# x + alpha * fx: other piece sizes, fx ahead of x, other buffer homes, the first store issued earlier

## The chip, the core and the metric

The kernel runs on one core of a Trainium2 chip. The metric is the device time of one execution in microseconds; the kernel before has a median of 150.96 us in 3 runs (150.96 to 151.07).

## What is computed

```python
B, S, D = 512, 32, 640
x, fx : bfloat16 [512, 32, 640]      alpha : bfloat16 [1]

def reference(x, fx, alpha):
    return x + alpha * fx
```

Two inputs of 20.97 MB are read and one output of 20.97 MB is written. There is one multiplication and one addition for each element.

## The kernel before

Each of the three large arrays is seen as 128 rows of 160 KiB, one row for each partition of the on-chip memory (SBUF). All pieces are counted in units of 1 KiB of such a row (K = 512 bfloat16 elements), so a row has N = 160 units. A piece of *n* units is one DMA with 128 rows of *n* KiB. In the trace each row of a DMA is one packet on one of 16 DMA engines, so each engine moves 8 rows of each DMA.

The on-chip buffer `buf` (L72 before and after) has ALL = 207 units. Both inputs together have 320 units, so they don't fit at once and places are used again.

- `X` and `F` list the pieces of x and fx as (first unit, end). In the kernel before, piece i of x always lies in `buf` at its own units, and piece j of fx at `HOME[j]`. Later pieces overwrite places where a fx piece has been used up.
- `C` lists the compute steps. A step multiplies its part of fx by alpha in place (VectorE `tensor_scalar`, L99) and adds it to x in place (VectorE `tensor_tensor`, L107). `CUT` cuts the addition of step 5 into a first part of 1 unit and the rest.
- `S` lists the stores: 64, 64 and 32 units.
- `PLAN` is an order written out by hand, in which instructions are issued. Loads, alpha's load and stores are all issued by SyncE (SP) on one DMA queue, so that a load that must wait for VectorE holds up everything that SP issues behind it. VectorE carries out its own instructions in PLAN's order too.
- `LATE` adds one wait by hand: store 0 is not issued before the first part of compute step 5.
- alpha is loaded as one element (third DMA), spread to 128 partitions by one small matmul, and copied to `a_f` by VectorE, which the multiplications use.

Five large loads (8, 56, 64, 30 and 49 units) and alpha are issued without a wait. The four loads behind them wait until VectorE has used up what they overwrite.

Of the kernel before, what the change touches and what calls it, by code (L numbers as in the profile page):

```python
# [1 line left out]

# [4 lines left out]

ACT = mybir.ActivationFunctionType
ALU = mybir.AluOpType
F32 = mybir.dt.float32  # L10
BF16 = mybir.dt.bfloat16

K = 512
P = 128

X = [(0, 8), (8, 64), (64, 94), (94, 126), (126, 160)]  # L20
F = [(0, 64), (64, 113), (113, 140), (140, 160)]
HOME = [94, 158, 160, 187]
C = [(0, 32), (32, 64), (64, 66), (66, 93), (93, 113), (113, 140), (140, 160)]
CUT = {5: 114}
S = [(0, 64), (64, 128), (128, 160)]
N = 160
ALL = 207

PLAN = """
x 0  # L30
x 1
a
f 0
x 2
f 1
c 0
x 3
c 1
c 2
x 4  # L40
c 3
f 2
c 4
f 3
c 5
c 6
s 0
s 1
s 2
"""  # L50
LATE = {("s", 0): ("c", 5)}


@with_exitstack
def kernel(
    ctx: ExitStack,
    tc: tile.TileContext,
    x: bass.AP,
    fx: bass.AP,
    alpha: bass.AP,  # L60
    out: bass.AP,
):
    nc = tc.nc
    xv = x.flatten_outer_dims().rearrange("(p n) d -> p (n d)", p=P)
    fxv = fx.flatten_outer_dims().rearrange("(p n) d -> p (n d)", p=P)
    ov = out.flatten_outer_dims().rearrange("(p n) d -> p (n d)", p=P)
    assert xv.shape[1] == N * K

    consts = ctx.enter_context(tc.tile_pool(name="consts", bufs=1))
    psum = ctx.enter_context(tc.tile_pool(name="psum", bufs=1, space=bass.MemoryType.PSUM))  # L70
    whole = ctx.enter_context(tc.tile_pool(name="whole", bufs=1))
    ctx.enter_context(tc.manual_schedule())  # L72

    sync = mybir.DependencyInfo(mybir.DependencyClass.Sync, mybir.DependencyReason.DATA)
    buf = whole.tile([P, ALL * K], x.dtype, name="buf")
    moved = {}
    done = []

    def transfer(what, out, in_):
        r = nc.sync.dma_start(out=out, in_=in_)  # L80
        if what in LATE:
            tc.add_manual_dep(r.ins, moved[LATE[what]].ins.name, sync, reason="issue late")
        moved[what] = r
        done.append(r)

    def load_x(i):
        a, b = X[i]
        transfer(("x", i), buf[:, a * K : b * K], xv[:, a * K : b * K])

    def load_f(j):  # L90
        (a, b), h = F[j], HOME[j]
        transfer(("f", j), buf[:, h * K : (h + b - a) * K], fxv[:, a * K : b * K])

    def compute(i):
        a, b = C[i]
        j = next(j for j, (s, e) in enumerate(F) if s <= a and b <= e)
        h = HOME[j] + a - F[j][0]
        term = buf[:, h * K : (h + b - a) * K]
        nc.vector.tensor_scalar(  # L99
            out=term, in0=term, scalar1=lanes["a_f"][:], scalar2=None, op0=ALU.mult  # L100
        )
        ends = [a, CUT.get(i, b), b]
        for s, e in zip(ends, ends[1:]):
            if s < e:
                term = buf[:, (h + s - a) * K : (h + e - a) * K]
                total = buf[:, s * K : e * K]
                r = nc.vector.tensor_tensor(out=total, in0=total, in1=term, op=ALU.add)  # L107
                moved.setdefault(("c", i), r)
                done.append(r)

    def store(i):
        a, b = S[i]
        transfer(("s", i), ov[:, a * K : b * K], buf[:, a * K : b * K])

    lanes = {}

    def alpha_to_lanes():
        a_1 = consts.tile([1, 1], alpha.dtype, name="a_1")
        transfer("a", a_1[:], alpha[None, :])
        ones = consts.tile([1, P], alpha.dtype, name="ones")  # L120
        nc.vector.memset(ones[:], 1.0)  # L121
        a_ps = psum.tile([P, 1], F32, name="a_ps")
        done.append(nc.tensor.matmul(a_ps[:], ones[:], a_1[:], start=True, stop=True))  # L123
        lanes["a_f"] = consts.tile([P, 1], F32, name="a_f")
        nc.vector.tensor_copy(out=lanes["a_f"][:], in_=a_ps[:])  # L125

    does = {"x": load_x, "f": load_f, "c": compute, "s": store, "a": alpha_to_lanes}
    for step in PLAN.split("\n"):
        if step:
            what, *of = step.split()  # L130
            does[what](*map(int, of))

    rest = nc.sync.nop(nofuse=True)
    for i in done[:-1]:
        tc.add_manual_dep(rest.ins, i.ins.name, sync, reason="all but the last store")


# [1 line left out]
_INS = ['x', 'fx', 'alpha']  # L139
_OUTS = [((512, 32, 640), 'bfloat16')]  # L140


# [23 lines left out]
```

## Time and profile before

| what | value |
|---|---|
| median of 3 runs | 150.96 us |
| span of the profiled execution | 149.4 us (149.42 in the trace) |
| outside the span (150.96 - 149.42) | 1.54 us |
| bytes moved | 62.92 MB, mean 421 GB/s over the span |
| time of packets on the 16 DMA engines | 97.9% of the span |
| VectorE busy | 66.6 us, 45% |

The trace has a record of every packet (start, duration, bytes). The table puts those of each DMA together, in the order of issue. "Floor" is the shortest duration of one row of that size in that DMA; "excess" is what all 128 rows took above the floor, divided by 16 engines; "longer" counts the rows that took over 20 ns more than the median of that DMA; "first" and "last" are when the first and the last of the 16 engines had finished its share, in us from the start of the span.

| DMA | KiB a row | floor, ns | excess, ns | longer | first engine done | last engine done |
|---|---|---|---|---|---|---|
| x 0 | 8 | 307 | 430 | 32 | 4.52 | 4.87 |
| x 1 | 56 | 2116 | 42 | 7 | 21.45 | 21.82 |
| fx 0 | 64 | 2418 | 13 | 1 | 40.80 | 41.20 |
| x 2 | 30 | 1138 | 42 | 11 | 49.88 | 50.51 |
| fx 1 | 49 | 1851 | 64 | 4 | 64.69 | 65.70 |
| x 3 | 32 | 1213 | 21 | 5 | 74.37 | 75.42 |
| x 4 | 34 | 1288 | 72 | 11 | 84.77 | 85.71 |
| fx 2 | 27 | 1022 | 62 | 7 | 92.95 | 93.88 |
| fx 3 | 20 | 761 | 30 | 5 | 99.16 | 99.95 |
| store 0 | 64 | 2418 | 98 | 23 | 118.87 | 119.27 |
| store 1 | 64 | 2418 | 41 | 0 | 138.23 | 138.59 |
| store 2 | 32 | 1213 | 24 | 0 | 147.94 | 148.27 |

How to read it: eight rows times the floor is the least time in which one engine can do its share of a DMA; the differences of the last column are the time that it took on whichever engine was last. The first row of the first DMA starts at 1.75 us, and the span ends 1.15 us after the last row.

### The profile page before, as it was taken

How to read it: one execution, taken by the hardware profiler on the slowest of the kernel's cores; microseconds unless marked ns; L12 is line 12 of the kernel's file. 1: busy time of each engine (PE TensorE's matmuls, PEld its weight loads, DVE VectorE, ACT ScalarE, POOL GpSimd, SP SyncE). 2: the span in 40 equal slices, each digit the busy share in tenths (PEclk: the TensorE clock that was granted, in tenths of full speed). 3: DMA queues.
4: the chain of work that ended last, by engine and by line, in shares of the span. 5: the costliest groups of instructions: out<-in, count | busy, mean ns of one | idle time of the engine just before them, and what ended most of it. 6: DMA issues, size and time to landing. Idle time of an engine off the chain costs nothing.

```text
span 149.4 us, 89 instructions
## 1 busy us (share of the span) xinstructions
PE 0.2 (0%) x1; PEld 0.1 (0%) x1; DVE 66.6 (45%) x17; POOL 0.2 (0%) x4
## 2 busy tenths in 40 slices
PE   0000000000000000000000000000000000000000
PEld 0000000000000000000000000000000000000000
DVE  0000000000089999999999970799994000000000
POOL 0000000000000000000000000000000000000000
DMA  5996996969899999979989999999696969696993
GB/s 184 588 445 292 491 526 281 561 298 544 379 428 395 548 430 443 416 312 447 470 382 419 431 451 417 433 495 544 298 561 281 561 281 561 281 561 281 509 465 149
DMA packets 1730, 62.92 MB, mean 421 GB/s; under 512 B 194, under 2 KB 194, under 8 KB 194
## 3 DMA queue, kind: packets, MB, share of 16 engines
q1 hardware_dynamic: 1730, 62.92, 97.9%
HBM read 41.94 MB, written 20.97 MB: 421 GB/s over the span
## 4 chain that ended last, share of the span: by engine, by line
DVE 38%; DMA 36%; issue 2%; SPq 1%; DVEq 0%
DMA buf<-in_fx_dram 36%; DVE buf L107 24%; DVE buf L99 13%; SPq L80 1%; DVEq L99 0%
## 5 line engine op out<-in xcount | busy, mean ns | idle before, releaser
L107 DVE TENSOR_TENSOR buf<-buf 128x16384 bf16<-128x16384 bf16 (+5 forms) x8 | 43.9, 5492 | 0.2
L99 DVE TENSOR_SCALAR buf<-buf,a_f 128x16384 bf16<-128x16384 bf16 (+3 forms) x7 | 22.8, 3264 | 24.9 <-DMA buf<-in_fx_dram 24.9
L125 DVE COPY a_f<-a_ps 128x1 f32<-128x1 f32 x1 | 0.2, 159 | 21.3 <-PE a_ps L123 21.3
L121 DVE MEMSET ones<- 1x128 bf16 x1 | 0.2, 165 | 0.8 <-PEq L150 0.8
L123 PE MATMUL a_ps<-a,ones 1*128 1x1 bf16 x1 | 0.2, 158 | 22.1 <-DMA a<-in_alpha_dram 22.1
L150 POOL MEMSET const-bfloat16-1.0<- 128x1 bf16 x1 | 0.1, 102 | 0.0
L150 POOL MEMSET const-uint8-127<- 128x1 uint8 x1 | 0.1, 102 | 0.0
L123 PEld LDWEIGHTS <-ones 1*128 1x128 bf16 x1 | 0.1, 100 | 1.0 <-DVE ones L121 1.0
L150 POOL MEMSET const-float32-0.0<- 128x1 f32 x1 | 0.1, 99 | 0.2 <-issue 0.2
L150 POOL MEMSET const-float32-1.0<- 128x1 f32 x1 | 0.1, 99 | 0.0
## 6 DMA issues: line engine op xcount, KB each, us to landing
buf<-in_x_dram SPq DMA_DIRECT2D x1, 7168.0 KB, 21.0
buf<-in_fx_dram SPq DMA_DIRECT2D x1, 6272.0 KB, 63.2
buf<-in_x_dram SPq DMA_DIRECT2D x1, 4352.0 KB, 16.9
buf<-in_x_dram SPq DMA_DIRECT2D x1, 4096.0 KB, 20.8
out_dram<-buf SPq DMA_DIRECT2D x1, 4096.0 KB, 34.8
buf<-in_x_dram SPq DMA_DIRECT2D x1, 3840.0 KB, 48.5
buf<-in_fx_dram SPq DMA_DIRECT2D x1, 3456.0 KB, 14.0
buf<-in_fx_dram SPq DMA_DIRECT2D x1, 2560.0 KB, 11.8
```

What stands on the lines that cost most here:

```text
L80: r = nc.sync.dma_start(out=out, in_=in_)
L99: nc.vector.tensor_scalar(out=term, in0=term, scalar1=lanes["a_f"][:], scalar2=None, op0=ALU.mult)
L107: r = nc.vector.tensor_tensor(out=total, in0=total, in1=term, op=ALU.add)
L121: nc.vector.memset(ones[:], 1.0)
L123: done.append(nc.tensor.matmul(a_ps[:], ones[:], a_1[:], start=True, stop=True))
L125: nc.vector.tensor_copy(out=lanes["a_f"][:], in_=a_ps[:])
L150: nc = _bacc.Bacc("TRN2", target_bir_lowering=False, num_devices=1)
```

## The change

The pieces, the order and the places in `buf` are new; the arithmetic, the number of DMAs (9 loads, alpha, 3 stores) and the stores' sizes stay.

- x is loaded in 64, 32, 32, 32 units, fx in 8, 56, 32, 32, 32. Each piece carries its own home as a third number, for x too.
- The first two DMAs load fx (8 and 56 units) in place of x; x's first 64 units come behind them.
- Six loads of 32 units follow in the order fx, x, fx, x, fx, x. The first two of them wait for nothing. The other four wait for an addition that uses up the place they overwrite: fx 3 for the total of 32 to 64, x 2 for 0 to 32, fx 4 for 79 to 96, x 3 for 111 to 128.
- VectorE multiplies 64, 32, 32 and 32 units and adds in 7 pieces (32, 32, 17, 15, 17, 15, 32 units).
- `LATE` is gone. Store 0 stands in SP's order behind x 3, and waits for nothing that SP has not waited for already.

```diff
-X = [(0, 8), (8, 64), (64, 94), (94, 126), (126, 160)]
-F = [(0, 64), (64, 113), (113, 140), (140, 160)]
-HOME = [94, 158, 160, 187]
-C = [(0, 32), (32, 64), (64, 66), (66, 93), (93, 113), (113, 140), (140, 160)]
-CUT = {5: 114}
+F = [(0, 8, 96), (8, 64, 104), (64, 96, 160), (96, 128, 128), (128, 160, 175)]
+X = [(0, 64, 0), (64, 96, 64), (96, 128, 96), (128, 160, 143)]
 S = [(0, 64), (64, 128), (128, 160)]
 N = 160
 ALL = 207
 
 PLAN = """
+f 0
+f 1
+a
 x 0
+f 2
 x 1
-a
-f 0
+m 0 64
+t 32 64
+t 0 32
+f 3
 x 2
-f 1
-c 0
+m 64 96
+t 79 96
+f 4
+t 64 79
+m 96 128
+t 111 128
 x 3
-c 1
-c 2
-x 4
-c 3
-f 2
-c 4
-f 3
-c 5
-c 6
+t 96 111
+m 128 160
+t 128 160
 s 0
 s 1
 s 2
 """
-LATE = {("s", 0): ("c", 5)}
...
+    def units(v, a, b):
+        return v[:, a * K : b * K]
+
+    def at(pieces, a, b):
+        s, _, h = next(p for p in pieces if p[0] <= a < p[1])
+        e, _, g = next(p for p in pieces if p[0] < b <= p[1])
+        assert h - s == g - e
+        return units(buf, a + h - s, b + h - s)
...
+    def multiply(a, b):
+        term = at(F, a, b)
+        done.append(
+            nc.vector.tensor_scalar(
+                out=term, in0=term, scalar1=lanes["a_f"][:], scalar2=None, op0=ALU.mult
+            )
+        )
...
+    def total(a, b):
+        s = at(X, a, b)
+        done.append(nc.vector.tensor_tensor(out=s, in0=s, in1=at(F, a, b), op=ALU.add))
...
+    def store(i):
+        a, b = S[i]
+        done.append(nc.sync.dma_start(out=units(ov, a, b), in_=at(X, a, b)))
```

(m a b is `multiply`, t a b is `total`; f, x, s and a are the loads, the stores and alpha as before.)

## The prediction

> **What bounds the kernel now.** I began with the page's head and its DMA rows.
>
> ```profile
> span 149.4 us, 89 instructions
> PE 0.2 (0%) x1; PEld 0.1 (0%) x1; DVE 66.6 (45%) x17; POOL 0.2 (0%) x4
> ...
> q1 hardware_dynamic: 1730, 62.92, 97.9%
> HBM read 41.94 MB, written 20.97 MB: 421 GB/s over the span
> ```
>
> VectorE (DVE) works less than half of the span; the one DMA queue is occupied for 97.9% of it. What is left to the queue is 2.1%, some 3.1 us. Stretches cut where DMAs end show where it is:
>
> ```profile
> 0.00:1.74 1.74, 0.00 (x0) 0.10 (x1) 0.17 (x1) 0.20 (x4) 1.00 0.00 0
> ...
> 148.28:149.40 1.12, 0.00 (x0) 0.00 (x0) 0.00 (x0) 0.00 (x0) 1.00 0.00 0
> ...
> 40.80:99.20 58.40, 0.00 (x0) 0.00 (x0) 51.62 (x13) 0.00 (x0) 1.00 1.00 431
> 99.45:147.90 48.45, 0.00 (x0) 0.00 (x0) 14.41 (x3) 0.00 (x0) 1.00 1.00 431
> ```
>
> The last two numbers are the DMA share and GB/s. Nothing moves for the first 1.74 us or the last 1.12; in between the engines are full, in the loads as in the stores. (Packets are counted whole where they start, so only long stretches can be compared.) Then the timeline, for whether the queue ever waits for its issuer:
>
> ```profile
> 54.89 14.58 SPq L80 DMA_DIRECT2D buf<-in_x_dram  x2
> ...
> 80.27 8.65 SPq L80 DMA_DIRECT2D buf<-in_fx_dram  x2
> ...
> 98.60 15.66 SPq L80 DMA_DIRECT2D out_dram<-buf  x3
> ```
>
> The second number spans from the first issue of the group to the end of its last. x 3 is issued at 54.89, before fx 1 ahead of it has finished (65.70 in the table by DMA); fx 2 at 80.27, x 4 ends at 85.71. Store 0 is issued at 98.60, when the first engine finishes its loads at 99.16, and its first rows start at 99.44: here alone some engines stand still. The chain of waits explains VectorE's order only; it ends at 113.9, 35 us before the span, with the additions:
>
> ```profile
> 105.57 2.81 DVE buf L99
> 108.38 0.02 issue
> 108.40 5.49 DVE buf L107
> ```
>
> So the end is set by the bytes: on each engine 96 rows, one behind the other. The floors in the table lie on one line: 64 and 32 KiB differ by 2418 - 1213 = 1205 ns, 37.66 ns per KiB, and 1213 - 32 x 37.66 = 8 ns go to each row; 20 KiB gives 761 by this line, as measured. An engine's whole floor is 480 KiB x 8 x 37.66 ns = 144.6 us plus 96 x 8 ns = 0.8, together 145.4; the first row starts at 1.75 and the span ends 1.15 after the last, together 148.3. The span of 149.42 has only 1.1 us above that, which bounds any gain.
>
> **Where this 1.1 us is.** About 0.66 us lies in the first DMA: 1.75 to 4.87 is 3.12 us, 8 rows of 307 are 2.46. From fx 0's end to the last store's, the last engine needs 148.27 - 41.20 = 107.07; eight times the floors of those nine DMAs (1138, 1851, 1213, 1288, 1022, 761, 2418, 2418, 1213) is 106.58. So 0.49 us are lost. By the column of the last engine, x 2 takes 9.31 against 9.10 and fx 1 15.19 against 14.81, together 0.59 above the floor; the rest are between 0.02 under and 0.02 over. The engines, 0.40 apart at 41.20, are 1.01 apart at 65.70: single rows take up to 276 ns longer, on some engine. This befalls the loads of 30, 49, 34, 27 and 20 KiB (excess 42, 64, 72, 62, 30 ns) more than those of 64 (13) and 32 KiB (21).
>
> **The change, part by part.**
>
> 1. *Startup.* The first two DMAs have 8 and 56 KiB rows as before, alpha is third, a 64 KiB load fourth. fx for x is the same shape: 0. All are issued before 3.4 us and the last engine is done with them at 41.20 again; bounds -0.1 to +0.1, from the spread of the three runs (0.11).
> 2. *Row sizes.* Behind that, before: 30+49+32+34+27+20 = 192 units in six loads; after: six of 32. Bytes, rows and DMAs are the same, so the floors are as well: 58.20 and 58.20. What can change is the loss. x 3, the one 32 KiB load of the trace, cost the last engine 75.42 - 65.70 = 9.72. Six such: 41.20 + 6 x 9.72 = 99.52 against 99.95: **-0.43 us**. Lower bound: no loss at all, 6 x 9.70, -0.55. Upper bound: every one loses as x 2 did (0.21), 6 x 9.91 = 59.46, end at 100.66, +0.71. I take x 3's own row, because it has the size.
> 3. *Store 0 without LATE.* It is issued behind x 3, far ahead of need (below). The gap goes away: engines done at 99.16 waited until 99.44. But the last engine, done at 99.95, went on at once, and it is the one that ends the kernel, so 0; bounds -0.12 (the idle time summed over 16 engines and divided by 16, if they shared their rate) and +0.05 (their wait also brought the engines closer together).
> 4. *New homes and waits.* They cost nothing while each load is issued before the one ahead has ended. VectorE by its rows: 16384 elements take 4.48 us in L99 and 8.69 in L107, 10240 take 2.88 and 5.49; by these lines a multiplication of 32768 takes 8.76, additions of 8704 and 7680 take 4.69 and 4.16 (estimates). A DMA's data were seen 0.45 us after its last row (41.20, L99 starts at 41.65).
>    - The multiplication of 0 to 64 waits for fx at 21.82 and for a_f at 22.5: done at 31.3, long before x 0 (41.20).
>    - Additions 32-64 and 0-32 end at 50.3 and 59.0. fx 3 is issued at 50.4 (x 1 ahead of it ends at 60.6), x 2 at 59.1 (fx 3: 70.4).
>    - Multiplication 64-96 to 63.5, addition 79-96 to 68.2: fx 4 is issued at 68.3 (x 2: 80.1). Addition 64-79 to 72.4, multiplication 96-128 to 76.9.
>    - Addition 111-128 waits for x 2 (80.1 + 0.45) and ends at 85.2; x 3 is issued then, its first row could start 1.0 later (at the start 0.73 to 1.75), and fx 4 ends at 89.8. This cover, 3.6 us, is the thinnest. Queued behind x 3 on SP are all three stores.
>    - Store 0 is issued at 85.7 (x 3: 99.5), store 1 after addition 96-111 at 89.4 (store 0 ends at 118.8), store 2 after the last addition, 100.0 + 8.7 = 108.7 (138.2).
> 5. *Fewer VectorE instructions*, 4 + 7 for 7 + 8: by the lines above 66.0 us for 66.6. Hidden: VectorE ends at 108.7, its last result is needed at 138.2. 0.
>
> Sum: the last row ends at 99.52 + 19.32 + 19.32 + 9.68 = 147.84 for 148.27, the span is 147.84 + 1.15 = 148.99, -0.43. With the 1.54 us that lie between span and median, **150.53 us**; its own range is 150.40 to 150.70.
>
> **Rivals.**
>
> *A: the stretched rows don't depend on the size (no change, 150.96).* They came with the first VectorE work at 41.65, and fx 0, x 1 and the stores, with few of them, lie mostly outside that work; then the same bytes of VectorE work stretch the new rows as well, 0.49 us again. Against it: between 88.56 and 94.29 VectorE was idle, and 3 of the 79 rows wholly in idle stretches behind 41 us were longer, by 291 ns together (3.7 ns for each of the 79); of 641 rows wholly beside its work 37, by 2932 (4.6 each). The two are close. The Trainium skill (SBUF — State Buffer, "SBUF: two separate sides") says that a DMA can't be slowed by a compute operation, as the two use separate ports; this trace agrees, by 3.7 against 4.6 ns, and by that rule A loses its VectorE half. What is left of A is chance: a few long rows that fall on any engine at any size.
>
> *B: aligned rows disturb each other (slower, 151.7).* All loads now start and end at multiples of 32 KiB of their rows but for the first cut; if engines in step then hit the same memory at once, each of the six loads loses what x 2 did, 0.21: the upper bound above, +0.71, 151.67. It turns to a loss once each load loses over (99.95 - 41.20 - 58.20) / 6 = 0.09. For it: the losses are already there and not understood. Against: fx 0 and store 1, at 0 and 64 KiB with the engines in step, have 1 and 0 longer rows. The Trainium skill (DMA: Bandwidth & Descriptors, "Latency and other measured facts") tells of copies that lose half of their rate where the rows lie a large power of two apart; here rows lie 160 KiB apart before and after, and no run here shows such a loss.
>
> *C: the queue runs dry before x 3 (slower, 151.6).* If addition 111-128 or what precedes it ends over 3.6 us later, all engines stand still for the rest; with that addition at twice its time (+4.7) 1.1 us, less the 0.43: 151.6. Against: all additions of the trace lie on one line, at 8.69 and 5.49.
>
> **How the numbers follow.** Forecast 0.55, A 0.25, B 0.12, C 0.08. A measurement of this kernel can tell 0.2%, 0.30 us, from no change: the borders are 150.66 and 151.26. The forecast stays under 150.66 in some nine of ten (0.50), else it counts as the same (0.05). A lies within in four of five (0.20), with 0.02 faster and 0.03 slower; B and C are slower (0.20). Together 0.52, 0.25 and 0.23. The range runs from 150.30, just under the lower bounds together (-0.55 and -0.12), to 151.30, which takes in A; outside are most of B and C and little at the lower end, under 0.2.
>
> **What would show it.** Right: last-engine ends near 99.5 for x 3 and 147.8 for store 2, the engines no more than 0.6 us apart at the end of each load, few rows over 20 ns longer, store 0's rows starting the moment x 3's end, x 3 issued near 85. Wrong: excess over 40 ns per 32 KiB load (A), over 0.09 us on the last engine in each (B), or an idle stretch of all engines about 90 us (C); also a startup that ends elsewhere than at 41.2.

## The result and the profile after

The changed kernel takes 151.67 us (median of 5 runs, 151.53 to 151.81), the kernel before 151.04 us beside it: a ratio of 1.0039, 95% interval 1.0027 to 1.0051. It is slower by 0.4%, where it was forecast to be faster by 0.3%.

The page of the changed kernel, its head and the rows on the DMA queue:

```profile
span 149.9 us, 84 instructions
PE 0.2 (0%) x1; PEld 0.1 (0%) x1; DVE 65.9 (44%) x13; POOL 0.2 (0%) x4
...
q1 hardware_dynamic: 1730, 62.92, 98.0%
HBM read 41.94 MB, written 20.97 MB: 420 GB/s over the span
```

The engines are as full as before (98.0% of a span that is 0.5 us longer), and VectorE has 0.7 us less to do. So no time was lost in waiting; the same packets took longer. Where, the chain of waits gives away. It shows start, length and what:

```profile
59.34 21.44 DMA buf<-in_x_dram
...
85.59 15.24 DMA buf<-in_x_dram
100.83 0.03 issue
...
100.92 8.69 DVE buf L104
```

x 3, the last load, is issued at 85.59, near the 85.2 that was forecast, and its data are seen at 100.83 instead of 99.97. The timeline has the store right behind it:

```profile
85.59 0.33 SPq L92 DMA_DIRECT2D buf<-in_x_dram  x1
86.02 23.96 SPq L108 DMA_DIRECT2D out_dram<-buf  x3
```

Three stretches around the end of that load (the last three columns are the granted clock, DMA share and GB/s; a packet is counted whole where it starts):

```profile
89.40:96.70 7.30, 0.00 (x0) 0.00 (x0) 4.72 (x2) 0.00 (x0) 1.00 1.00 431
96.70:99.10 2.40, 0.00 (x0) 0.00 (x0) 0.00 (x0) 0.00 (x0) 1.00 1.33 437
99.10:101.90 2.80, 0.00 (x0) 0.00 (x0) 0.98 (x1) 0.00 (x0) 1.00 0.87 375
```

In the middle one two rows start on each engine, 32 in all (437 GB/s). They occupy 1.33 of the stretch where they should fill 1.01 of it: the same bytes, a third more time. VectorE does nothing meanwhile.

The records of single rows say the same for each DMA. "Before again" is a second profile of the kernel before (run e5 below), "held back" is run e1, the changed kernel with its first store issued later. Columns as in the table of the profile before; the 56 KiB load and store 1 are left out.

| DMA, before / after | before again: excess, ns | last engine done | after: excess | last engine done | held back: excess | last engine done |
|---|---|---|---|---|---|---|
| 1st, 8 KiB | 667 | 5.31 | 595 | 5.28 | 607 | 5.28 |
| 64 KiB | 5 | 41.55 | 8 | 41.50 | 6 | 41.50 |
| 30 / 32 KiB | 0 | 50.63 | 0 | 51.18 | 0 | 51.18 |
| 49 / 32 | 25 | 65.65 | 3 | 60.88 | 5 | 60.88 |
| 32 / 32 | 22 | 75.33 | 20 | 70.59 | 28 | 70.58 |
| 34 / 32 | 30 | 85.61 | 30 | 80.31 | 29 | 80.29 |
| 27 / 32 | 25 | 93.79 | 28 | 90.02 | 30 | 90.00 |
| last load, 20 / 32 | 32 | 99.85 | **785** | **100.47** | 30 | 99.74 |
| store 0, 64 | 84 | 119.17 | 0 | 119.79 | 70 | 119.08 |
| store 2, 32 | 24 | 148.20 | 0 | 148.79 | 23 | 148.18 |

Up to 90 us the loads follow each other as forecast, but for a start that ends 0.3 us later (41.50 for 41.20). In the last load 28 of 128 rows, all of them among the last two of their engine, start between 96.8 and 98.7 us and take 93 to 645 ns more than 1213. From there on everything is late by the same 0.6 us.

### The profile page after: what moved, and what is told of

Its sections match the earlier page's. It is cut to its first block, busy times and chain, and to the rows that moved or that the text cites. A ratio compares the mean times of both kernels' runs of the same rounds, so it can differ in the third digit from the quotient of the medians.

```text
span 149.9 us, 84 instructions
## 1 busy us (share of the span) xinstructions
PE 0.2 (0%) x1; PEld 0.1 (0%) x1; DVE 65.9 (44%) x13; POOL 0.2 (0%) x4
## 4 chain that ended last, share of the span: by engine, by line
DMA 51%; DVE 20%; SPq 1%; issue 0%; DVEq 0%
DMA buf<-in_x_dram 51%; DVE buf L104 20%; SPq L88 1%; SPq L112 0%; DVEq L104 0%
## 5 line engine op out<-in xcount | busy, mean ns | idle before, releaser
L104 DVE TENSOR_TENSOR buf<-buf 128x16384 bf16<-128x16384 bf16 (+2 forms) x7 | 43.5, 6251 | 20.5 <-DMA buf<-in_x_dram 20.5
L97 DVE TENSOR_SCALAR buf<-buf,a_f 128x16384 bf16<-128x16384 bf16 (+1 forms) x4 | 22.2, 5550 | 0.9 <-DMA buf<-in_fx_dram 0.9
```

The costliest lines, as they stand in the source:

```text
L97: nc.vector.tensor_scalar(out=term, in0=term, scalar1=lanes["a_f"][:], scalar2=None, op0=ALU.mult)
L104: done.append(nc.vector.tensor_tensor(out=s, in0=s, in1=at(F, a, b), op=ALU.add))
```

## The experiments

Theory T1: a store that stands in the queue behind the last load stretches that load's last rows. Rival R1: something else at that place does.

**e1, the changed kernel with store 0 held back.** The addition of 96 to 111 is cut and moved behind the last multiplication, as a clock for the store:

```diff
-t 96 111
 m 128 160
+t 96 109
+t 109 111
 t 128 160
...
+LATE = {0: (96, 109)}
...
+        if i in LATE:
+            tc.add_manual_dep(r.ins, made[LATE[i]].ins.name, sync, reason="issue late")
```

> The changed kernel with store 0 held back until an addition of 13 units ends (by its rows near 98.7 us); for that the addition of 96 to 111 is cut into 13 and 2 units and stands behind the last multiplication. Theory T1 (a store that stands in the queue behind the last load stretches that load's last rows): the last load's excess falls from 785 ns an engine to under 60, its last engine ends near 99.8 in place of 100.47, the time falls by 0.5 to 0.75 us to 150.9 to 151.2. Rival R1 (the rows at 96.8 to 99.2 us are stretched by something else, as the position in the queue or the places in the buffer): excess stays near 785, time stays 151.5 to 151.8.

Measured: 151.07 us, ratio to the kernel before 0.9998 [0.9989, 1.0007]. The stretches of this run:

```profile
89.40:96.70 7.30, 0.00 (x0) 0.00 (x0) 6.19 (x2) 0.00 (x0) 1.00 1.00 431
96.70:99.10 2.40, 0.00 (x0) 0.00 (x0) 2.40 (x2) 0.00 (x0) 1.00 1.01 437
99.10:101.90 2.80, 0.00 (x0) 0.00 (x0) 1.64 (x2) 0.00 (x0) 1.00 1.04 445
```

The same 437 GB/s of rows now fill 1.01 of the stretch, though VectorE works all through it. In the chain the load takes 14.62 us from issue to data in place of 15.24:

```profile
85.58 14.62 DMA buf<-in_x_dram
100.20 0.03 issue
```

T1 holds; the excess falls from 785 to 30 ns.

**e2, the kernel before without its wait by hand**, the converse, at other row sizes and places:

```diff
-LATE = {("s", 0): ("c", 5)}
+LATE = {}
```

> The kernel before without its one wait by hand, so that store 0 is issued near 89 us, behind the last load of 20 KiB rows. T1: rows of that last load are stretched on all engines, excess from 30 ns to 500 to 800, time from 151.0 to 151.4 to 151.7. R1: excess stays under 80 ns, time 150.9 to 151.1.

Measured: 151.54 us, 1.0027 [1.0017, 1.0038]; excess of the last load 501 ns, done at 100.28. Its timeline, its stretch, and the same stretch of the kernel before again (e5):

```profile
89.45 16.44 SPq L80 DMA_DIRECT2D out_dram<-buf  x2
```

```profile
96.70:99.10 2.40, 0.00 (x0) 0.00 (x0) 2.37 (x3) 0.00 (x0) 1.00 0.96 341
```

```profile
96.70:99.10 2.40, 0.00 (x0) 0.00 (x0) 2.37 (x3) 0.00 (x0) 1.00 0.98 418
```

With the store in the queue from 89.45, engines that are as busy move 341 GB/s (second fence), where they move 418 with the store issued at 98.53 (third fence). One line of the old kernel, its `LATE`, is worth 0.4 us.

**e3 and e4, x in the first DMA again**, without and with the store held back. In the profile of the kernel before the first DMA had ended at 4.87, in the changed kernel at 5.28 us; T2 puts it down to the array that is read first.

```diff
-F = [(0, 8, 96), (8, 64, 104), (64, 96, 160), (96, 128, 128), (128, 160, 175)]
-X = [(0, 64, 0), (64, 96, 64), (96, 128, 96), (128, 160, 143)]
+F = [(0, 64, 96), (64, 96, 160), (96, 128, 128), (128, 160, 175)]
+X = [(0, 8, 0), (8, 64, 8), (64, 96, 64), (96, 128, 96), (128, 160, 143)]
...
```

The order follows: x's 8 units, fx's 64 units, alpha, x's other 56 units, then as in the changed kernel.

> The changed kernel with the first DMA (8 units) and the third large one (56 units) loading x and the second (64 units) fx, the rest as it is. Theory T2 (the first DMA's later end, 5.28 for 4.87 us, comes from what it reads or where it puts it): first DMA ends near 4.9, the time falls by 0.3 to 0.4 us to 151.3. Rival R2 (the start differs from one execution to the next): first DMA ends anywhere from 4.8 to 5.4, and the median stays within 0.15 us of 151.67.

> Both edits of the two runs before on the changed kernel: held-back store 0 and x in the first DMA. T1 and T2 together: 150.5 to 150.7, the first version under the kernel before. T1 and R2: 150.9 to 151.1. R1 and R2: 151.5 to 151.8.

Measured: 151.60 us (1.0033 [1.0021, 1.0046]) and 151.16 us (1.0003 [0.9994, 1.0012]). The first DMA ends at 5.34 and 5.25 with x in it. T2 falls. The pair shows T1 once more: 544 against 30 ns in the last load.

**e5, the kernel before unchanged, for a second profile.**

> The kernel before unchanged, for a second profile. Theory T4 (the long rows between 41 and 100 us, and the first DMA's end at 4.87, belong to the one execution that was profiled, not to the row sizes): the first DMA ends near 5.3 on its last engine, and the five odd loads have an excess under 40 ns each, as they had without the wait by hand. Rival R4 (they come with these row sizes while store 0 is held back): excess 40 to 70 ns again, first DMA near 4.9.

Measured: the same time (1.0004 [0.9994, 1.0014]). Its first DMA ends at 5.31, and its loads of 30 to 20 KiB have an excess of 0 to 32 ns (table above). T4 holds: the early start and the long rows were those of one execution. In the first profile they all but offset each other, since its last row ended at 148.27, and at 148.20 in e5.

**e6, e9, e10: the cut of the first 64 units**, with the store held back as in e1: uncut, 2 + 62, 16 + 48. The second of them, beside e1's edit:

```diff
-F = [(0, 8, 96), (8, 64, 104), (64, 96, 160), (96, 128, 128), (128, 160, 175)]
+F = [(0, 2, 96), (2, 64, 98), (64, 96, 160), (96, 128, 128), (128, 160, 175)]
```

> The changed kernel with store 0 held back and with fx 0 of 64 units in one DMA, not cut into 8 and 56. T5 (the 0.6 us that the first DMA loses above its floor are lost in any case): fx 0 ends near 22.1, time 151.0 to 151.1, the same within 0.1. R5 (they are lost to the many small first rows): fx 0 ends near 21.5, time 150.4 to 150.7. R6 (the cut spares something): fx 0 ends above 22.5, time 151.4 and more.

> The changed kernel with store 0 held back and fx's first 64 units cut into 2 and 62 in place of 8 and 56. T6 (the smaller the first piece, the less is lost at the start; 64 uncut lost 0.84 us, 8 lost 0.6 to 0.75): the first 64 units end at 21.9 or earlier for 22.17, time 150.75 to 150.95, under the kernel before. R7 (8 is small enough, the loss is the first rows' own): 22.1 to 22.3, time 151.0 to 151.15.

> The same with 16 and 48 units. T6: the first 64 units end between 22.2 and 22.5, time 151.1 to 151.3. R7: as with 8, 22.1 to 22.25, time 151.0 to 151.15.

Measured:

| first piece, KiB a row | first 64 units done on the last engine | us | ratio to before |
|---|---|---|---|
| 2 | 22.39 | 151.32 | 1.0015 [1.0006, 1.0024] |
| 8 (e1) | 22.19 | 151.07 | 0.9998 [0.9989, 1.0007] |
| 16 | 22.37 | 151.07 | 1.0003 [0.9994, 1.0012] |
| 64 (uncut) | 22.57 | 151.46 | 1.0028 [1.0016, 1.0039] |

R6 holds for the uncut load: the cut spares 0.4 us. T6 falls: it put 2 KiB under 151 us, and it takes 151.32, against 151.07 with 16 KiB beside it; 8 and 16 can't be told apart by the time. Rows that run at the start take up to 1.4 us longer when they have 64 KiB, up to 0.98 when they have 8; why a middle size is best stays open.

**e7, e12: how late is late enough.** As e1, with the store issued at 95.30 and at 97.22:

```diff
-LATE = {0: (96, 109)}
+LATE = {0: (96, 97)}
...
-t 96 109
-t 109 111
+t 96 97
+t 97 111
```

(e12 cuts at 105.)

> The changed kernel with store 0 held back only until near 95.4 us (an addition of 1 unit behind the last multiplication), before the last two rows of the last load start on each engine (96.8). T1a (what counts is that the store stands in the queue when the last two rows run): excess of the last load 500 to 800 ns, time 151.5 to 151.7. T1b (it must have stood there since before the load began): excess under 100 ns, time 151.0 to 151.1.

> The changed kernel with store 0 held back until near 97.5 us, when the last row but one of the last load runs on each engine and the last has not started. T8 (a store in the queue stretches each row that starts while it stands there): only the last rows are stretched, excess 250 to 450 ns, time 151.2 to 151.5. R10 (both last rows have to start behind it): excess under 60 ns, no idle stretch before store 0, 150.9 to 151.05.

Measured for e7: 151.52 us (1.0031 [1.0019, 1.0042]), excess 402 ns; for e12: 150.81 us beside 150.87 of the kernel before (0.9995 [0.9986, 1.0004]), excess 23 ns, and store 0's rows start at 99.13, when the first engine ends its loads, so that none stands still. In the timelines:

```profile
95.30 14.49 SPq L113 DMA_DIRECT2D out_dram<-buf  x3
```

```profile
97.22 11.85 SPq L113 DMA_DIRECT2D out_dram<-buf  x3
```

In e1 the store's first row ran 0.86 us after its issue, so the stores of e7 and e12 stood in the queue from about 96.2 and 98.1 (estimates). In e7 the rows that began between 96.8 and 97.3 are not stretched; of the 16 last ones, from 98.07 on, 14 are. In e12 the last ones begin between 97.92 and 98.24 and are not. So T1a holds against T1b, though its excess of 500 to 800 was too high. T8 falls, as the last rows but one of e7 began behind the store and kept their length; R10 fits both runs. A store that came about one row before the end (e12) did no harm, one that came some two and a half rows before it (e7) did; nothing between was tried. On this one queue only about the last two rows of the load are at risk: in the changed kernel the first six rows on each engine were not stretched, though the store was issued at 86.02 us. How many of the two it takes varies: of the 16 last rows but one, 12 were stretched there, 3 in e3 and none in e8 (next run), with the store issued equally early. One profile of each can't say why.

**e8, store 0 cut into 8 and 56 units**, both issued early:

```diff
-S = [(0, 64), (64, 128), (128, 160)]
+S = [(0, 8), (8, 64), (64, 128), (128, 160)]
```

> The changed kernel with store 0 cut into 8 and 56 units, both issued early as in it; one DMA more. T1c (the loss goes with the bytes of the store's first rows that are fetched ahead): excess of the last load falls from 785 to under 300 ns, time 151.1 to 151.3. T1d (it goes with the store as such): excess 500 to 800, time 151.6 to 151.8.

Measured: 151.68 us (1.0040 [1.0028, 1.0053]), excess 450 ns. The excess of 450 lies between T1c's (under 300) and T1d's (500 to 800). It is less than 785, but e3 with its uncut store has 544, and the time is T1d's: T1c finds no support.

**e11, store 0 on ScalarE's DMA queue**, so that its rows run among the loads' rows:

```diff
+        queue = nc.scalar if i == 0 else nc.sync
+        done.append(queue.dma_start(out=units(ov, a, b), in_=at(X, a, b)))
```

> The changed kernel with store 0 issued by ScalarE on a second DMA queue as soon as its additions are done (near 59 us), so that its rows run between the rows of the loads for tens of us. T7 (each meeting of a load's row and a store's row on an engine stretches both, by what the last two rows of the last load lost, some 0.3 us a row): 8 store rows an engine among loads add 2 to 5 us, 153 to 156. R8 (the loss is paid once, where the queue turns from loads to stores): 151.4 to 151.9. R9 (it is paid only on one queue): 150.9 to 151.1.

Measured: 153.21 us (152.28 to 153.82), 1.0151 [1.0121, 1.0180]. The timeline of ScalarE's queue has the issue, the stretches show where the time goes:

```profile
59.15 0.37 ACTq L109 DMA_DIRECT2D out_dram<-buf  x1
```

```profile
60.00:64.00 4.00, 0.00 (x0) 0.00 (x0) 3.97 (x2) 0.00 (x0) 1.00 1.22 401
64.00:84.00 20.00, 0.00 (x0) 0.00 (x0) 8.31 (x2) 0.00 (x0) 1.00 1.01 434
```

The time falls in T7's range, but not by its mechanism. Where the store comes in, between 60 and 64 us, the 39 load rows take 1.18 us longer for each engine; for the 20 us behind that rows of both kinds run side by side at 434 GB/s; near the end of the stretch that they share (88.3 us) and where store 1 meets the last load another 0.1 and 0.3 us are lost. It is the turns that cost, not the mixture. R8 and R9 fall as well: the loss is paid more than once, and not on one queue only.

The rows where the store comes in add something to T1. No row of the store has moved when the first load rows are stretched: the store is issued at 59.15, the stretched rows start from 60.30 on, the first store row at 63.75. On all 16 engines it is just the last two load rows ahead of the engine's first store row that are stretched, by 0.7 to 1.5 us together; the rows ahead of those are 21 ns over 1213 at most. So it is again about two load rows in front of a waiting store, here on another queue and in the middle of the loads.

## Why the prediction was wrong

**What bounds the kernel** was right: the bytes do. The row floors held (1213 and 2418 ns, within 3 ns, in all runs), no queue ran dry, and but for e11 (2.3 us) all differences here are fractions of a microsecond.

**Part 1, startup, 0: right as a difference, wrong as a time.** The first DMA ends at 5.31 in the kernel before again and at 5.28 in the changed one, the third large load at 41.55 and 41.50. But the forecast built on 41.20, with bounds of 0.1, and named another end as a sign of being wrong; it came 0.30 later. The bounds were too tight for one profile against another: 4.87 and 5.31 are two executions of one kernel. e6 and e9 show that the start is worth up to 0.4 us, to a change of the first cut; this change kept it.

**Part 2, row sizes, -0.43: wrong, a failed step; it measured 0.** It took the 0.49 us of long rows for a property of the loads of 30, 49, 34, 27 and 20 KiB. e5 shows them gone at the same sizes, and e2 has an excess of 0 to 36 ns in the five loads from 30 to 27 KiB. The gain was read from one execution, in which an early start made up for the long rows. The 32 KiB loads did run as forecast (0 to 30 ns), but there was nothing to win: with the store held back, e1, e4, e10 and e12 are between 0.9995 and 1.0003 of the kernel before.

**Part 3, store 0 without LATE, 0, bounds -0.12 to +0.05: wrong, the failed step that made the kernel slower.** By e1 against the changed kernel it is (1.0039 - 0.9998) x 151.04 = 0.62 us, by e2 0.41 us. In the trace of before the store came in at the very end, issued 0.56 us before the first engine was done with the loads; no row of it showed a store waiting behind a load. The step priced only the gap that goes away and took the price of an early store to be nothing. This was an unseen condition of the queue, and its bound should have been as wide as the other unknowns.

**The sum.** From 148.99 to 149.89 the span is off by 0.90 us: the start +0.30, the five loads behind it -0.08, the last load +0.73 (10.45 us on the last engine for 9.72), the stores 0.00, the end -0.05. The other 0.24 of the miss is the term for what lies outside the span. The 1.54 us set the span of one execution against the median of others; for the changed kernel it is 151.67 - 149.89 = 1.78, and 1.7 to 1.8 in all runs that have both figures. So the profile of before belonged to an execution of about 151.2 us (an estimate, 149.42 + 1.78), some 0.2 above its own median; up to that much of the 0.49 us that the change was to win back may not have been in the median at all.

**Parts 4 and 5: right.** Loads were issued at 50.7, 59.3, 68.5 and 85.6 us for a forecast of 50.4, 59.1, 68.3 and 85.2, and the thinnest cover held. VectorE took 65.9 us for 66.0.

**The rivals.** A, no change, is what the new sizes and homes did. Its VectorE half is not needed: e1's loads run beside VectorE's work with 0 to 30 ns of excess, as the Trainium skill has it (SBUF — State Buffer, "SBUF: two separate sides"). B gave 151.67, the very figure that came out, but by chance. The time isn't lost in each aligned load: five of six lose nothing, and the sixth loses nothing either when the store is late. So the rule on rows a large power of two apart (the Trainium skill, DMA: Bandwidth & Descriptors, "Latency and other measured facts") has no part in it, and no run here shows such a loss. C did not happen.

**What stays open:** what an engine does with the waiting store in the last two rows. Loads behind loads have an excess of 0 to 30 ns in the same queue, so it takes a store, or the change from reading memory to writing it; which of the two, no run here separates. e11 shows that the queue need not be the same. e12 is not told apart from the kernel before, so no version beats both; it beats the changed kernel.

## What to carry to other kernels

When a queue is full from end to end, a wait that looks idle may be holding something back: before taking it out, ask what will stand in the queue earlier, and behind what. Here the first store did no harm when it was issued 0.6 to 2 us before the first engine ended the last load (the kernel before, e1, e12, which can't be told apart by the time), but did at 4 us (e7) and at over 13 (the changed kernel). And losses of a few tenths of a microsecond in single rows of one profile need a second profile of the same kernel before they are costed.

## What was not expected of the hardware

- A store queued behind a load stretches about the last two rows of the load on 14 to 16 of the 16 engines, by 402 to 785 ns an engine in the mean (five kernels), at 20 and at 32 KiB a row.
- Rows of loads and stores on two queues share the engines at 434 GB/s, but the turn into that state cost 1.18 us, in the last two load rows ahead of each engine's first store row.
- Two executions with an early first DMA (4.87 in the first profile of before, 5.01 in e12) have long rows in the loads that follow; the eight others with a first DMA of 8 KiB and one queue, which end it at 5.24 us or later, have few or none in the loads between the start and the last one. Why is not known.
